# A state-space scan and a squared-ReLU FFN on one core: two weight loads re-ordered among GpSimd's work, and the third block's down-projections written closer behind its up-projections

## The chip, the cores and the metric

The kernel runs on one core of one Trainium2 chip. The metric is device time in microseconds (us) for one execution; lower is better. Four compute engines take part, each with its own queue of instructions that it works off in order: TensorE (matmuls; PE in the profile, its weight loads PEld), VectorE (DVE), ScalarE (ACT) and GpSimd (POOL). SyncE (SP) computes nothing; it issues most of the DMA transfers, also in order. GpSimd issues the weight loads.

## What is computed

For each of 4 batches and 8 heads, a decayed linear recurrence runs over 768 positions; its output, 3072 rows of 256, goes through a feed-forward layer. Cut to what matters:

```
log_a = log(clip(a, 1e-6, 1))
for each chunk of 32 positions:
    cum   = cumsum(log_a)                      # within the chunk
    M     = (C @ B.T) * exp(cum_i - cum_j) * causal
    y     = M @ x  +  (C @ state) * exp(cum)
    state = exp(sum(log_a)) * state  +  (B * exp(cum_last - cum)).T @ x
h   = relu(y_rows @ w_in)                      # w_in: 256 x 2048
out = (h * h) @ w_out                          # w_out: 2048 x 256
```

The inputs are float32; the matmuls run on bfloat16. The chunk length of the reference is not kept: the kernel works in longer pieces.

## The kernel before

**Units.** The work is cut into 12 units, one for each batch and each third (256 positions) of the sequence, numbered 0 to 11 over the batches first. A unit is loaded as three tiles, C, B and x (`ph_load`, line 123), and prepared: C and B, scaled by the running products of a, are written side by side into a bfloat16 tile `jt` (`prep_c`, line 169, and `prep_b`, line 177), and x is multiplied by the inverse products into `xs` (`prep_x`, line 189). The products stand in `P_sb`, their inverses in `Pinv`; `inv` (line 648) fills `Pinv` a few columns at a time with reciprocals on VectorE. `jt` is transposed into `bct`: by TensorE for units 0 to 3 (line 207, copied out of PSUM at lines 220 and 222), by a DMA transpose that SyncE issues for units 4 to 11 (`dma_tr`, line 198).

**A unit on TensorE.** The scores of a unit (`ph_mt`, line 231 or 237) fill PSUM banks 0 to 3 and are masked into `mts` (line 246; some are copied by ScalarE at line 251 and masked at line 255). Then come the unit's own state contribution (`ph_u`), the part inside the unit (`ph_intra`) and the carry from earlier states (`ph_carry`); all three are matmuls at line 262. The carry reads `Sd`, a state times its decay, which GpSimd makes at line 378 (`ph_sd`) or VectorE at line 390 (`ph_sd_first`). ScalarE copies the state contribution to `us` (lines 343 and 346). From unit 4 on, one region `rg` does this in a fixed order: carry of the unit before, state contribution of the new one, inside part of the unit before, scores of the new one. `rg4` is the first of them: it finishes unit 3 and starts unit 4. Its first matmuls are the carry of unit 3.

**The feed-forward layer.** The 256 rows of one unit form a block, called a to l (a belongs to unit 0). A block has 8 up-chunks of 256 hidden columns, in ORDER written `a0` to `a7`: four matmuls with `w_in` at line 453, then a relu by ScalarE (line 474). `qa0` squares the chunk on VectorE (line 480). The capital `A0` is the down-chunk: four matmuls with `w_out`, also at line 453, which add into one accumulator bank for the block (bank 6 for block b, bank 7 for the others). Down-chunk 7 comes last in every block, and with it goes the block's end: `mm2(blk, 7)` is followed at once by `ph_out`, which puts a ScalarE copy of the accumulator (line 502) and an output store on SyncE (line 503) into the queues.

**The order.** Nothing is scheduled by a planner. The string `ORDER` (line 48) is a list of tokens, read from left to right; each token emits its instructions to its engine, and that is the order in which each engine works. Tokens that the text below needs, beside the chunks: `ld`, `ldC5:s` and so on, loads on SyncE; `wi0` to `wi3` and `wo0` to `wo3`, the four loads each of `w_in` and `w_out` by GpSimd (lines 150 and 154), each holding the weights of two chunks; `iv`, reciprocals into `Pinv`; `pc`, `pb`, `px`, the preparations of C, B and x; `tr`, the transpose; `tc`, its copies; `mt`, scores; `mk`, `sc`, `ms`, masks; `u`, `in`, `ca`, `sf`, `us`, `t`, the parts of a unit (state contribution, inside part, carry, first decayed state, and the copies to `us` and to `T`, the block's input); `sa`, decayed states on GpSimd; `id`, filler matmuls on ones (line 554) that keep TensorE busy while nothing else is ready. A number behind `@` picks the PSUM bank; without it the next free bank in turn is taken. The loads of a unit wait for nothing but a free buffer, or a small gate that VectorE or GpSimd writes.

In the stretch that matters here, TensorE works through blocks a, b and c while units 2 to 4 are loaded and prepared. The helper `after` (line 670) lets GpSimd copy one column of a loaded tile, so that what GpSimd issues next comes behind that load.

Of the kernel before, what the change touches and what calls it, by code (L numbers as in the profile page):

```python
# [10 lines left out]
FP32 = mybir.dt.float32  # L11
# [12 lines left out]
def _dap(base: bass.AP, offset_elems: int, dims):  # L24

    return bass.AP(tensor=base.tensor, offset=base.offset + offset_elems,
                   ap=[list(d) for d in dims])
# [3 lines left out]
def kernel(  # L31
# [15 lines left out]
    NU = 12  # L47
    ORDER = """
        fa1:a jz0:v ef jz1:p id3:512 ti fa0:s la0:s id4:512 pi eb ldB0:s ac0:v ldC0:a sk0 ku sp la1:a pbh0:p hd
        id1:256 pc0:v pbl0:v mb:a id2:512 trC0 ps iv:8:16 tcC0:1:a tcC0:0:v trB0 la2:s tcB0:2:v pk id1:512 iv1:0:8  # L50
        id1:512 ldx0:s mt0 wi0 la3:s px0:v ldC1:s su id2:512 ldB1:s wi1 ldx1:s u0:67 mk0 fq mk0 gC2:v mk0 ac1:v pc1:p sc0
        pb1:a jz2:a id2:512 tr1 id3:512 tc1:1:a tc1:0:v to ms0:p sf0 sk1 wo0 wi2 px1:p mt1 ina0 inb0 ca0 pp1:a mk1 mk1 t0:aa
        sc1 us0 mk1 fr p2@4 a0 ldC2:s a1 u1::6 ina1 ms1:v wo1 wi3 pc2 inb1 sf1 ca1 pd t1:va us1 a3@0 qa1 ldB2:s
        qa0 a2@1 wo2 b0@2 qa3 qb0 b1@3 qb1 b2@4 b3@5 A0 A1 B0 pb2:p B1 tr2 zb0 qb3 gB3:v ldx2:s ldB3:s ldC3:s ldx3:s b4 a4
        iv:32:64 zb1 tc2:1:v qa2 tc2:0:v b5 sb1 sb0 qb4 a5 qb2 qa4 mt2 sc2 B3 iv:16:32 px2 pc3 wo3 px3 mk2 mk2 sc2 A3
        A2 ms2:v ms2:v qa5 a6 b6 pb3:a B2 a7 qb5 qa6 b7 u2 ina2 inb2 sf2 ld4 A4 tr3 ca2 tc3:1:v t2:aa B4 us2 B5
        tc3:0:v u3:45 pc4 mt3 A5 us3 sc3 c5 qb7 qb6 mk3 za3 pb4 ldC5:s ldB5:s c3 qa7 c4 qc5 c0 qc3 px4 tr4 ldx5:s pb5
        pc5 sa3 c1 c6 ldC6:s tr5 ldB6:s ldx6:s qc4 qc0 A6 px5 pq A7 wm c2 B6 c7 C0 ms3:v mk3 qc6 mk3 qc7 afC2 pc6 B7
        C3 C6 C4 qc1 bk rg4 C1 qc2 d1 d0 za4 sa4 pb6 mk4 mk4 d3 mk4 C5 d4 qd0 d2 mk4 px6 tr6 ld7 C2 C7 qd1 qd2 qd3 zb3
        rg5 sb3 D0 mk5 za5 sa5 D1 mk5 d5 qd4 D2 pc7 pb7 d6 qd5 d7 qd6 D3 zb2 e0 qd7 mk5 e1 qe0 sb2 D4 mk5 D5 tr7 ld8  # L60
        e2 qe1 D6 e3 qe2 ml px7 rg6 e4 D7 qe3 za6 sa6 zb6 mk6 e5 qe4 sb6 e6 qe5 e7 qe6 iv:64:96 mk6 E0 E1 E2 E3 ldC9:s
        ldB9:s px8 mk6 f0 qe7 E4 f1 qf0 pc8 E5 pb8 tr8 ldx9:s E6 mk6 f2 qf1 f3 qf2 E7 rg7 mk7 F0 f4 qf3 za7 F1 F2 f5
# [12 lines left out]
    const = ctx.enter_context(tc.tile_pool(name="const", bufs=1))  # L75
# [29 lines left out]
    Pinv = const.tile([128, 2, 96], FP32, name="Pinv")  # L105
# [34 lines left out]
    def gate(k, what, eng=None):  # L140
        b, j = UNITS[k]
        w = {"B": N, "C": N, "x": D}[what]
        t = nat.tile([128, NH, 2 * w], FP32, tag=f"{what}_nat", name=f"{what}_nat{k}")
        loaded.setdefault(k, {})[what] = t
        (eng or nc.gpsimd).memset(t[:, 0, 0:1], 0.0)

    def load_w_in(i):
        f0, f1 = WIN[i]
        n = (f1 - f0) * 256
        nc.gpsimd.dma_start(out=w_in_b[i], in_=_dap(moe_w_in, f0 * 256, [[2048, 128], [128 * 2048, 2], [1, n]]))  # L150

    def load_w_out(i):
        f0, _ = WOUT[i]
        nc.gpsimd.dma_start(out=w_out_b[i].rearrange("p s d -> p (s d)"),
                            in_=_dap(moe_w_out, f0 * 65536, [[1024, 128], [1, 1024]]))
# [303 lines left out]
    def mm1(blk, fp, h=None):  # L459

        if h is None:
            h = bank()
        gi, o = group_of(WIN, fp)
        w = w_in_b[gi]
        for i in range(2):
            for g in range(2):
                col = g * w.shape[2] + (o // 2) * 512 + 2 * (o % 2) + i
                strips(pp[:, h, i * 256:(i + 1) * 256], lambda c, n: _fap(w, col + 4 * c, [[4, n]]),
                       T[blk][:, g].rearrange("p r u t -> p (r u t)"), start=(g == 0), stop=(g == 1))
        return h  # L470

    def relu(blk, fp, h):
        hb = fpool.tile([128, 2, 256], BF16, tag="hb", name=f"hb{blk}_{fp}")
        nc.scalar.activation(out=hb.rearrange("p i t -> p (i t)"), in_=pp[:, h, :], func=AF.Relu)  # L474
        hbs[(blk, fp)] = hb
# [59 lines left out]
    with tc.manual_schedule():  # L535
# [3 lines left out]
        V, P, A, SQ = nc.vector, nc.gpsimd, nc.scalar, nc.sync  # L539
# [111 lines left out]
        def first_a(u, eng):  # L651
            load_a(u, eng)
# [15 lines left out]
        def after(what, k):  # L668
            t = const.tile([128, 1], FP32, name=f"gate_{what}{k}")
            P.tensor_copy(out=t, in_=loaded[k][what][:, 0, 0:1])  # L670

        def order_load(k, what):
            gate(k, what)

# [88 lines left out]
        def one(t):  # L763
            t, _, w = t.partition("@")
            want[:] = [int(h) for h in w]
            f = t.split(":")
            name = f[0].rstrip("0123456789")
            k = int(f[0][len(name):] or 0)
            if len(name) == 1 and name.lower() in "abcdefghijkl" and len(f[0]) == 2:
                blk = "abcdefghijkl".index(name.lower())  # L770
                if name.islower():
                    relu(blk, k, mm1(blk, k))
                else:
                    mm2(blk, k)
# [7 lines left out]
            {  # L782
                "a": lambda: None,
                "fa": lambda: first_a(k, eng),
                "la": lambda: late_a(k, eng),
                "ldC": lambda: load(k, "C", eng, f[1] if len(f) > 2 else None),
                "ldB": lambda: load(k, "B", eng, f[1] if len(f) > 2 else None),
                "ldx": lambda: load(k, "x", eng, f[1] if len(f) > 2 else None),
                "ld": lambda: load_all(k),
                "gC": lambda: gate(k, "C", eng), "gB": lambda: gate(k, "B", eng), "gx": lambda: gate(k, "x", eng),  # L790
                "afC": lambda: after("C", k), "afB": lambda: after("B", k), "afx": lambda: after("x", k),
                "wi": lambda: load_w_in(k), "wo": lambda: load_w_out(k),
                "id": lambda: idle(k, f[1], dep(f[2]) if len(f) > 2 else None),
                "ef": lambda: eye(eye_f, ones_f), "eb": lambda: eye(eye_b, ones_b[:, 0:128]), "wm": warmed, "hd": head_rows,
                "jz": lambda: cleared(jt[k], eng), "ti": triangle, "ml": later_mask, "pi": picks, "ku": quads,
                "mb": lambda: causal(eng), "pk": picked, "ac": lambda: clamp(k, eng), "sk": lambda: scan(k), "sp": first_p, "pp": lambda: second_pick(eng),
                "su": first_sums, "to": first_total, "fq": first_quad, "p": lambda: second_p(), "pd": second_copy, "pq": second_quad,
                "ps": lambda: A.copy(out=P_sb[:, :, 0:32], in_=P0.rearrange("p (r c) -> p r c", r=2)),
                "iv": lambda: inv(int(f[1]), int(f[2]), k == 1),
                "pc": lambda: prep_c(k, eng or P, P0 if k == 0 else None),  # L800
                "pb": lambda: prep_b(k, eng or P), "pbl": lambda: prep_b(k, eng, (0,)), "pbh": lambda: prep_b(k, eng, (1,)),
                "px": lambda: prep_x(k, eng or P),
                "tr": lambda: transpose(k, "") if k < 4 else dma_tr(k),
                "trC": lambda: transpose(k, "C"), "trB": lambda: transpose(k, "B"),
                "tc": lambda: trc(k, "", f[1], eng), "tcC": lambda: trc(k, "C", f[1], eng), "tcB": lambda: trc(k, "B", f[1], eng),
                "mt": lambda: scores(k), "mk": lambda: mask_direct(k) if k < 4 else next_mask(k), "sc": lambda: score_copy(k),
                "ms": lambda: mask_copied(k, eng),
                "u": lambda: first_u(k, f[1] if len(f) > 1 else None, f[2] if len(f) > 2 else None), "sf": lambda: ph_sd_first(k),
                "ca": lambda: ph_carry(k, live[k]["h"], live[k]["begun"]),
                "in": lambda: intra(k, ""), "ina": lambda: intra(k, "a"), "inb": lambda: intra(k, "b"),  # L810
                "t": lambda: region_t(k, f[1]), "us": lambda: region_us(k),
                "cm": lambda: cols.append(True), "rg": lambda: rg(k), "bk": late_banks, "fr": lambda: busy.discard(4),
                "za": lambda: ph_z(k, 0), "zb": lambda: ph_z(k, 1), "sa": lambda: ph_sd(k, 0), "sb": lambda: ph_sd(k, 1),
            }[name]()
# [59 lines left out]
```

## Time and profile before

| | us |
|---|---|
| median of 3 runs | 113.69 |
| lowest and highest | 113.65, 114.04 |
| the profiled execution | 113.69 |
| its span, first to last instruction | 112.0 |
| TensorE busy in it | 107.1 |
| VectorE, ScalarE, GpSimd busy | 83.0, 77.0, 49.3 |

The profile is one execution seen by the hardware profiler. A row of a timeline gives the start and the length in us from the span's start, the engine, the line of the kernel, the operation, output `<-` inputs, how many instructions are merged, and in brackets how long the engine stood idle before and what released it. The release is inferred: of several things waited for, the one that came last by the profile is named. Matmuls overlap, so a row's length holds the end of its last matmul; the distance between the starts of two rows is the time that the work takes. A transfer has two times, the time that its issue takes on the queue of its engine, and the time from issue to landing.

### The profile page before, as it was taken

Reading aid. Unit: us, or ns where it says so; the run is one execution under the profiler, and the core shown is the slowest. Engines: PE = TensorE matmul, PEld = TensorE weight load, DVE = VectorE, ACT = ScalarE, POOL = GpSimd, SP = SyncE. Lnnn points to the kernel's source line nnn. Section 1 sums busy time; section 2 is a strip of 40 time slices with the busy share of each in tenths; the row PEclk is TensorE's granted clock in tenths of the full one; section 3 lists DMA queues with packets and bytes.
Section 4 is the critical chain, followed back from the end, with each engine's and each line's share of the span. In section 5 each row is a group of like instructions: output and inputs, shape, how many; then the busy total and the mean of one; then the engine's idle time right before and its main releaser. Section 6 shows DMA issues by size and latency. Waiting matters only on the chain.

```text
span 112.0 us, 3688 instructions
## 1 busy us (share of the span) xinstructions
PE 107.1 (96%) x1453; PEld 91.8 (82%) x1453; DVE 83.0 (74%) x190; ACT 77.0 (69%) x159; POOL 49.3 (44%) x95
## 2 busy tenths in 40 slices
PE   6989999999899999999999999999999999999990
PEld 2436789878798989989989989899899899899980
DVE  1799768998973999979967998679598298355440
ACT  1767994876974776695677776877876867867840
POOL 7599464097565473494083960665420020000000
PEclk9999999999999999999999999999999999999999
DMA  1999999999689799998888877888940020010203
GB/s 37 202 208 136 184 205 216 165 200 186 98 173 119 81 288 77 130 162 89 118 152 115 187 110 85 189 102 113 168 117 0 6 97 0 33 61 6 94 0 94
DMA packets 67281, 13.44 MB, mean 120 GB/s; under 512 B 63104, under 2 KB 65984, under 8 KB 67264
## 3 DMA queue, kind: packets, MB, share of 16 engines
q1 hardware_dynamic: 64320, 10.88, 60.4%
q0 software_dynamic: 1664, 2.10, 11.6%
q10 hardware_dynamic: 1280, 0.23, 1.1%
q8 instruction: 11, 0.18, 0.7%
q14 instruction: 6, 0.05, 0.1%
HBM read 10.58 MB, written 3.15 MB: 123 GB/s over the span
## 4 chain that ended last, share of the span: by engine, by line
PE 72%; DMA 14%; POOL 5%; DVE 4%; issue 1%; SPq 1%; ACT 0%; POOLq 0%; ACTq 0%
PE pp L453 64%; DMA w_out_b<-in_moe_w_out_dram 11%; PE pp L262 5%; DMA B_nat<-in_B_dram 3%; PE pp L231 2%; DVE h L480 2%; POOL jt L169 2%; POOL w_in_b L150 1%; POOL xs L189 1%; DVE mts L246 1%; POOL mts L255 1%; PE pp L237 1%; DVE bct L222 1%; SPq L656 0%; SPq L119 0%
## 5 line engine op out<-in xcount | busy, mean ns | idle before, releaser
L474 ACT ACTIVATE hb<-pp 128x512 bf16<-128x512 f32 x96 | 54.5, 603 | 22.5 <-PE pp L453 20.6
L480 DVE TENSOR_TENSOR h<-hb 128x512 bf16<-128x512 bf16 x96 | 45.1, 486 | 13.2 <-ACT hb L474 12.9
L453 PE MATMUL pp<-w_out_b,h 128*128 128x256 bf16 (+1 forms) x400 | 53.8, 268 | 0.6 <-DMA w_out_b<-in_moe_w_out_dram 0.4
L453 PE MATMUL pp<-T,w_in_b 128*128 128x256 bf16 x384 | 53.3, 273 | 0.0
L453 PEld LDWEIGHTS <-w_in_b 128*128 128x128 bf16 x384 | 41.4, 114 | 1.8 <-issue 1.1
L453 PEld LDWEIGHTS <-h 128*128 128x128 bf16 x400 | 37.6, 98 | 5.4 <-issue 1.9
L246 DVE TENSOR_TENSOR mts<-pp,mask 128x512 bf16<-128x512 f32 x43 | 28.5, 676 | 0.8 <-PE pp L231 0.8
L189 POOL TENSOR_TENSOR xs<-x_nat,Pinv 128x256 bf16<-128x256 f32 (+1 forms) x19 | 13.8, 739 | 13.4 <-PE pp L262 4.6
L378 POOL TENSOR_TENSOR Sd<-z,Pquad 128x256 bf16<-128x256 f32 x16 | 10.6, 669 | 12.9 <-DVE z L362 8.9
L169 POOL TENSOR_TENSOR jt<-C_nat,P_sb 128x128 bf16<-128x128 f32 x22 | 9.8, 466 | 9.6 <-DMA C_nat<-in_C_dram 9.4
L362 DVE SCALAR_TENSOR_TENSOR z<-z,Ptot,us 128x64 f32<-128x64 f32 x8 | 3.0, 371 | 6.8 <-ACT us L346 4.6
L554 PE MATMUL pp<-const-bfloat16-1.0 128*128 128x512 bf16 (+1 forms) x19 | 6.4, 465 | 0.8 <-PEq L858 0.8
L502 ACT COPY osb<-pp 128x512 f32<-128x512 f32 x11 | 6.4, 583 | 1.0 <-PE pp L453 1.0
L177 POOL CAST jt<-B_nat 128x256 bf16<-128x256 f32 x9 | 4.1, 458 | 3.5 <-PE pp L453 3.2
L262 PE MATMUL pp<-mts,xs 64*32 64x128 bf16 (+1 forms) x288 | 5.4, 219 | 0.0
L262 PE MATMUL pp<-bct,Sd 128*128 128x128 bf16 x40 | 4.2, 220 | 0.3 <-DVE Sd L390 0.2
L262 PEld LDWEIGHTS <-xs 64*32 64x32 bf16 (+1 forms) x288 | 3.6, 93 | 0.4 <-issue 0.2
L262 PEld LDWEIGHTS <-Sd 128*128 128x128 bf16 x40 | 3.0, 98 | 0.9 <-DVE Sd L390 0.6
L554 PEld LDWEIGHTS <-const-bfloat16-1.0 128*128 128x128 bf16 x19 | 1.7, 112 | 2.4 <-issue 2.2
L150 POOL DMA_DIRECT2D w_in_b<-in_moe_w_in_dram x4 | 3.0, 759 | 0.2 <-issue 0.2
L251 ACT CAST sc<-pp 128x512 bf16<-128x512 f32 x5 | 2.9, 608 | 0.4 <-PE pp L237 0.3
L262 PEld LDWEIGHTS <-jt 64*32 64x32 bf16 (+1 forms) x128 | 1.5, 90 | 1.9 <-issue 0.8
(78 smaller groups left out, 57.7 us busy)
## 6 DMA issues: line engine op xcount, KB each, us to landing
out_dram<-osb SPq DMA_DIRECT2D x11, 256.0 KB, 2.9
x_nat<-in_x_dram SPq DMA_DIRECT2D x6, 256.0 KB, 4.9
w_in_b<-in_moe_w_in_dram POOLq DMA_DIRECT2D x4, 256.0 KB, 7.0
w_out_b<-in_moe_w_out_dram POOLq DMA_DIRECT2D x4, 256.0 KB, 6.8
B_nat<-in_B_dram SPq DMA_DIRECT2D x6, 128.0 KB, 4.4
C_nat<-in_C_dram SPq DMA_DIRECT2D x12, 64.0 KB, 3.5
B_nat<-in_B_dram SPq DMA_DIRECT2D x12, 64.0 KB, 2.9
x_nat<-in_x_dram SPq DMA_DIRECT2D x6, 128.0 KB, 2.9
```

The source lines that it names most:

```text
L150: nc.gpsimd.dma_start(out=w_in_b[i], in_=_dap(moe_w_in, f0 * 256, [[2048, 128], [128 * 2048, 2], [1, n]]))
L169: eng.tensor_tensor(out=_fap(jt[k % 3], 128 + 144 * g, [[384, 2], [32, 4], [1, 16]]), in0=_fap(loaded[k]["C"], 128 * g, [[16, 2], [32, 4], ...
L177: fn(out=_fap(jt[k % 3], 0, [[384, 2], [16, 2], [32, 4], [1, 16]]), in_=_fap(loaded[k]["B"], 0, [[16, 2], [128, 2], [32, 4], [1, 16]]))
L189: eng.tensor_tensor(out=_fap(xs, 256 * r, [[256, 2 // n], [32, 8], [1, 32]]), in0=_fap(loaded[k]["x"], 32 * r, [[32, 2 // n], [64, 8], [1, ...
L246: nc.vector.tensor_tensor(out=live[k]["mts"][:, q].rearrange("p r g i -> p (r g i)"), in0=pp[:, q, :], in1=mask1 if k >= LATE else mask, o ...
L262: nc.tensor.matmul(dst, w, v, start=bool(need), stop=False, skip_group_check=True, **({} if pos is None else {"tile_position": pos}))
L378: nc.gpsimd.tensor_tensor(out=_fap(S_d, 0, [[128, 2], [32, 4], [1, 32]]), in0=_fap(z, 0, [[32, 2], [0, 4], [1, 32]]), in1=_fap(Pquad, 4 * ...
L453: nc.tensor.matmul(dst, w(0, 128), v, skip_group_check=True, **flags)
L474: nc.scalar.activation(out=hb.rearrange("p i t -> p (i t)"), in_=pp[:, h, :], func=AF.Relu)
L480: nc.vector.tensor_tensor(out=h2, in0=hb, in1=hb, op=ALU.mult)
L502: nc.scalar.copy(out=osb, in_=pp[:, 6 if blk == 1 else 7, :])
L554: nc.tensor.matmul(pp[:, h, 0:int(cols)], ones_b[:, 0:128], ones_b[:, 0:int(cols)] if dep is None else dep, start=True, stop=True, skip_gr ...
```

## The change

Two lines of code are added, and tokens are moved in ORDER.

1. A new token `hold` stands ahead of `wi0`, the first load of `w_in`. It lets GpSimd copy one column of `Pinv`, column 8, which the reciprocals `iv:8:16` write.
2. One filler is shortened: `id2:512` (two matmuls of 512 columns) becomes `id1:384` (one of 384), ahead of the first unit's transposes.
3. `wo3`, the last load of `w_out`, moves ahead of `px2` (the third x) and `pc3` in GpSimd's order.
4. The chunks of blocks a, b and c are written in another order. A4, B4, A5 now stand ahead of unit 2's state contribution `u2`, then B5, A6, B6; A7 stands behind c0 and B7 behind c3. The up-chunks of block c go c0 c3 c4 c6 c5 c1 c2 c7, with banks given by `@`; C0, C3, C4 and C6 follow two up-chunks behind their own, and none of them is left between c7 and `rg4`. The squares move with them; `us3` is written ahead of the scores `mt3`.

With A7 and B7 their copies and stores move too: A7 from behind `ldx6` to ahead of `ldC5`, B7 from there to ahead of `tr4`.

The diff, with the unchanged lines around it left out:

```diff
-        id1:256 pc0:v pbl0:v mb:a id2:512 trC0 ps iv:8:16 tcC0:1:a tcC0:0:v trB0 la2:s tcB0:2:v pk id1:512 iv1:0:8
-        id1:512 ldx0:s mt0 wi0 la3:s px0:v ldC1:s su id2:512 ldB1:s wi1 ldx1:s u0:67 mk0 fq mk0 gC2:v mk0 ac1:v pc1:p sc0
+        id1:256 pc0:v pbl0:v mb:a id1:384 trC0 ps iv:8:16 tcC0:1:a tcC0:0:v trB0 la2:s tcB0:2:v pk id1:512 iv1:0:8
+        id1:512 ldx0:s mt0 hold wi0 la3:s px0:v ldC1:s su id2:512 ldB1:s wi1 ldx1:s u0:67 mk0 fq mk0 gC2:v mk0 ac1:v pc1:p sc0
...
-        iv:32:64 zb1 tc2:1:v qa2 tc2:0:v b5 sb1 sb0 qb4 a5 qb2 qa4 mt2 sc2 B3 iv:16:32 px2 pc3 wo3 px3 mk2 mk2 sc2 A3
-        A2 ms2:v ms2:v qa5 a6 b6 pb3:a B2 a7 qb5 qa6 b7 u2 ina2 inb2 sf2 ld4 A4 tr3 ca2 tc3:1:v t2:aa B4 us2 B5
-        tc3:0:v u3:45 pc4 mt3 A5 us3 sc3 c5 qb7 qb6 mk3 za3 pb4 ldC5:s ldB5:s c3 qa7 c4 qc5 c0 qc3 px4 tr4 ldx5:s pb5
-        pc5 sa3 c1 c6 ldC6:s tr5 ldB6:s ldx6:s qc4 qc0 A6 px5 pq A7 wm c2 B6 c7 C0 ms3:v mk3 qc6 mk3 qc7 afC2 pc6 B7
-        C3 C6 C4 qc1 bk rg4 C1 qc2 d1 d0 za4 sa4 pb6 mk4 mk4 d3 mk4 C5 d4 qd0 d2 mk4 px6 tr6 ld7 C2 C7 qd1 qd2 qd3 zb3
+        iv:32:64 zb1 tc2:1:v qa2 tc2:0:v b5 sb1 sb0 qb4 a5 qb2 qa4 mt2 sc2 B3 iv:16:32 wo3 px2 pc3 px3 mk2 mk2 sc2 A3
+        A2 ms2:v ms2:v qa5 a6 b6 pb3:a B2 a7 qb5 qa6 b7 qb6 A4 B4 A5 u2 ina2 inb2 sf2 ld4 B5 tr3 ca2 qb7 tc3:1:v t2:aa A6 us2 B6
+        tc3:0:v qa7 u3:45 pc4 us3 mt3 sc3 c0@4 mk3 za3 A7 pb4 ldC5:s ldB5:s c3@5 qc0 B7 c4@0 C0 qc3 c6@1 px4 tr4 ldx5:s pb5
+        pc5 sa3 qc4 C3 c5@4 wm qc6 ms3:v C4 c1@5 ldC6:s tr5 ldB6:s ldx6:s mk3 px5 pq c2@0 C6 qc5 mk3 c7@1 qc7 afC2 pc6
+        qc1 bk rg4 C1 qc2 d1 d0 za4 sa4 pb6 mk4 mk4 d3 mk4 C5 d4 qd0 d2 mk4 px6 tr6 ld7 C2 C7 qd1 qd2 qd3 zb3
...
+        def hold():
+            t = const.tile([128, 1], FP32, name="gate_inv")
+            P.tensor_copy(out=t, in_=Pinv[:, 0, 8:9])
...
+                "hold": hold, "wi": lambda: load_w_in(k), "wo": lambda: load_w_out(k),
```

More of the change, by code (lines that the diff above doesn't have):

```diff
@@ L791, in one @@
                 "afC": lambda: after("C", k), "afB": lambda: after("B", k), "afx": lambda: after("x", k),
-                "wi": lambda: load_w_in(k), "wo": lambda: load_w_out(k),
+                "hold": hold, "wi": lambda: load_w_in(k), "wo": lambda: load_w_out(k),
                 "id": lambda: idle(k, f[1], dep(f[2]) if len(f) > 2 else None),
```

## The prediction

> **What bounds the kernel now.** I read the page first, then the table of stretches, then TensorE's own timeline, and only then the queues that feed it. The profiled execution took 113.69 us, the same as the median of the three runs (113.65 to 114.04); its span is 112.0, so 1.69 us lie outside and I leave them as they are.
>
> ```profile
> span 112.0 us, 3688 instructions
> ```
> ```profile
> 36.00:112.00 76.00, 73.06 (x913) 66.35 (x912) 54.75 (x120) 52.55 (x103) 25.87 (x47) 1.00 0.62 99
> ```
>
> The second row is the stretch from 36 us to the end: TensorE (first pair) is busy 73.06 of 76.00 us at the full granted clock (1.00). Nothing waits there that could be given back, so a microsecond won or lost before 36 us is won or lost in the total. The change lies wholly before 36 us, so I read TensorE there. The columns are start, length, engine, line, form and count, with the idle time before and what ended it.
>
> ```profile
> 23.62 0.25 PE L262 MATMUL pp<-xs,jt 64*32 64x64 bf16 x16
> ...
> 26.82 0.61 PE L453 MATMUL pp<-w_out_b,h 128*128 128x256 bf16 x4
> 27.27 2.78 PE L453 MATMUL pp<-T,w_in_b 128*128 128x256 bf16 x24
> 30.50 1.03 PE L453 MATMUL pp<-w_out_b,h 128*128 128x256 bf16 x8 [0.45 <-DMA w_out_b<-in_moe_w_out_dram]
> ...
> 32.25 0.60 PE L453 MATMUL pp<-T,w_in_b 128*128 128x256 bf16 x4
> ...
> 34.87 0.28 PE L262 MATMUL pp<-bct,Sd 128*128 128x128 bf16 x2
> ...
> 35.58 0.42 PE L237 MATMUL pp<-bct 32*64 32x256 bf16 x16
> 35.94 0.61 PE L453 MATMUL pp<-w_out_b,h 128*128 128x256 bf16 x4
> ...
> 39.88 0.39 PE L262 MATMUL pp<-bct,Sd 128*128 128x128 bf16 x4
> ```
>
> One chunk of either projection is four matmuls; from 26.82 to 27.27 that is about 0.44 us. The 24 matmuls at 27.27 therefore occupy 2.62 us and TensorE could go on at 29.89; it goes on at 30.50. That 0.61 us is the wait for the last w_out, which GpSimd issues late:
>
> ```profile
> 24.47 5.99 DMA w_out_b<-in_moe_w_out_dram
> ```
> ```profile
> PE pp L262 <- DVE Sd L390: 0.2, 1, 0.2
> PEld L207 <- DVE jt L169: 0.2, 1, 0.2
> ```
>
> The first wait row is a second stall, a carry behind its decayed state (0.2 us). So this change has some 0.8 us to win in its second half.
>
> **Gains, and the small terms.** The third x is prepared on GpSimd after a long pause, and the state us3 is copied on ScalarE:
>
> ```profile
> 22.22 1.21 POOL L189 TENSOR_TENSOR xs<-x_nat,Pinv 128x512 bf16<-128x512 f32 x1 [3.32 <-DVE mts L255]
> ```
> ```profile
> 26.65 0.27 ACT L343 COPY us<-pp 128x128 f32<-128x128 f32 x1 [0.59 <-PE pp L262]
> ```
>
> The last w_out moves ahead of that x, from 24.47 to 18.90, where the pause of 3.32 begins. Landing 6 us later, at 25, it is there before A6, which now follows the region of unit 2 (23.62) and four chunks, so comes after 25.4: minus 0.61. B5 and the transposes now lie between the decayed state and its carry, about 0.8 us of cover: minus 0.2. The shorter filler is worth nothing: the transposes behind it already wait for VectorE (second wait row), and the 640 columns that go (0.27 us, by 0.44 for a chunk's 1024) are a shorter pause than the 0.45 us at 30.50, which the clock bore at 1.00. The written order puts c0, right behind the scores of unit 3, into the bank that us3 empties. us3 ended at 26.92, and TensorE, free at 26.82, would now wait for it: plus 0.16, with 0.06 for the semaphore (an estimate, between the 0.04 and the 0.1 from an end to the next engine's start further down).
>
> The hold makes GpSimd wait for the reciprocal and copy one column before the first w_in:
>
> ```profile
> 5.18 0.25 DVE L648 RECIPROCAL Pinv<-P_sb 128x16 f32<-128x16 f32 x1 [0.20 <-ACT P_sb L798]
> ```
> ```profile
> 5.37 1.63 POOL L150 DMA_DIRECT2D w_in_b<-in_moe_w_in_dram  x2 [0.24 <-issue]
> 7.14 0.76 POOL L169 TENSOR_TENSOR jt<-C_nat,P_sb 128x128 bf16<-128x128 f32 x2
> ...
> 36.05 0.19 POOL L670 COPY gate_C<-C_nat 128x1 f32<-128x1 f32 x1
> ```
> ```profile
> 7.69 0.40 ACT L177 CAST jt<-B_nat 128x256 bf16<-128x256 f32 x1 [0.73 <-DMA B_nat<-in_B_dram]
> ```
>
> The table is there at 5.43; plus 0.06 and a copy of 0.19 (line 670 copies the same one column) the first w_in starts at 5.7, or 5.95 if the 0.24 pause repeats: 0.3 to 0.6 later. Queued behind are the second w_in, the C preparation at 7.14 and everything GpSimd issues after. The second unit's transposes wait for the later of that preparation (7.90, now 8.2 to 8.5) and the B copy on ScalarE (8.09), so they move by 0.1 to 0.4. A gain is excluded, since the preparation cannot end earlier. I take plus 0.15: the first issue's share of the 1.63 may shrink behind the hold, which puts the low end nearer.
>
> So far: minus 0.61, minus 0.20, plus 0.16, plus 0.15, which is minus 0.50. TensorE would be ready for the fourth region (rg4, at 34.87) at 34.37.
>
> **The term that decides: two stores moved past SyncE's loads.** A7 and B7 each end a block, and the last chunk of a block also issues its ScalarE copy and its output store on SyncE. Before, A7 stood behind the x load of unit 6. Now A7 stands ahead of the C and B loads of unit 5, and B7 ahead of the transpose of unit 4. SyncE works in written order, and does wait for such copies:
>
> ```profile
> SPq L503 <- ACT osb L502: 22.3, 3, 7.6
> ```
> ```profile
> 25.29 1.98 SPq L136 DMA_DIRECT2D B_nat<-in_B_dram  x1
> 27.44 3.46 SPq L198 DMA_TRANSPOSE bct<-jt  x1
> 30.95 0.56 SPq L136 DMA_DIRECT2D x_nat<-in_x_dram  x1
> 31.57 1.33 SPq L131 DMA_DIRECT2D C_nat<-in_C_dram  x2
> ...
> 38.35 1.18 SPq L503 DMA_DIRECT2D out_dram<-osb  x2
> ```
>
> So the B load of unit 5, issued at 25.29 so far, must wait for the store of block A. When is that? From c0 to rg4 the new order has 14 chunks, 14 times 0.437 or 6.1 us: c0 at 28.25, A7 at 28.7, its result at 29.3 (a chunk's row lasts 0.60). ScalarE has c0's relu ahead of the copy. Before, the copy stood 0.04 behind the end of A7 (30.50 plus 1.03), and took 0.58:
>
> ```profile
> 31.57 0.58 ACT L502 COPY osb<-pp 128x512 f32<-128x512 f32 x1 [0.56 <-PE pp L453]
> ```
>
> It ends at 30.0. The store issues at 30.05 for 0.59 (half of 1.18), C at 30.65, B at 31.25. How long B then takes:
>
> ```profile
> DMA to landing us min/median/max: 3.0/3.1/3.3
> ```
> ```profile
> DMA to landing us min/median/max: 6.2/6.2/6.2
> ```
> ```profile
> DMA to landing us min/median/max: 2.6/2.8/2.9
> ```
>
> These are the first two B loads, when little else was under way; unit 5's B of 25.29, amid the weights; and unit 6's half-size B at 35 to 37. The queues will have drained by 30 us, as the loads stood still, so I take 3.1: landing 34.35, against 31.5 before. Who waits for it:
>
> ```profile
> 31.59 0.40 POOL L177 CAST jt<-B_nat 128x256 bf16<-128x256 f32 x1 [1.73 <-PE pp L453]
> ...
> 32.84 0.61 POOL L378 TENSOR_TENSOR Sd<-us,Pquad 128x256 bf16<-128x256 f32 x1
> ```
>
> GpSimd's copy started 0.1 after the landing, and 1.86 us after that the decayed state of unit 3 was ready (33.45), queued behind unit 5's two preparations. rg4's first matmuls are that state's carry, and TensorE cannot step over them. Now: 34.45, ready at 36.31, carry at 36.37. Against 34.87 that is **plus 1.50**, with the minus 0.50 already inside. The bounds: 2.6 us of flight and stores and loads that issue as quickly as the early ones give plus 0.4; 6.2 us would give plus 4.6, which an emptied queue makes unlikely.
>
> Inside this wait lies a second one, worth nothing while the first stands. c7 is now last before rg4, and c1's square is queued behind c7's on VectorE:
>
> ```profile
> 33.57 1.10 DVE L480 TENSOR_TENSOR h<-hb 128x512 bf16<-128x512 bf16 x3 [0.71 <-ACT hb L474]
> ```
>
> From c7's start (32.25) to the second of these squares (34.33) is 2.08 us; the work from c7 to C1 is 0.44 plus 1.07 (34.87 to 35.94). C1 would stand 0.62 with the semaphore, were rg4 on time.
>
> **The transpose and the next region.** The store of block B follows B's load, then the transpose of unit 4 at about 32.45 instead of 27.44. Transposes landed in:
>
> ```profile
> DMA to landing us min/median/max: 2.8/4.6/5.3
> ```
>
> That gives 37.05; the scores that read it come 0.71 into rg4, at 37.08. It just fits. SyncE then gets to unit 5's x and unit 6's C after 0 to 3.46 us more, C at 33.0 to 36.5 instead of 31.57. GpSimd waits for that C, and the carry of the fifth region stands behind it:
>
> ```profile
> 36.51 0.76 POOL L169 TENSOR_TENSOR jt<-C_nat,P_sb 128x128 bf16<-128x128 f32 x2 [0.27 <-DMA C_nat<-in_C_dram]
> 37.23 0.61 POOL L378 TENSOR_TENSOR Sd<-z,Pquad 128x256 bf16<-128x256 f32 x1
> ```
>
> Its state, ready at 37.84 so far, moves by 1.4 to 4.9, to 39.2 to 42.7; the carry would be due at 39.88 plus 1.5, 41.4. A wait of 0 to 1.3; I take 0.3. Sum: 1.50 and 0.30 are **plus 1.8, 115.5 us**.
>
> The Trainium skill (DMA: Bandwidth & Descriptors, section Anatomy of one DMA) fits a transfer, for GpSimd's issues, as 2.0 us plus its bytes at 436 GB/s. For 128 KB that is an estimate of 2.3 us, and the sum by it would be plus 1.0, 114.7. The first B loads took 3.0 to 3.3 here, so I stay with the row.
>
> **Rivals.** (1) Not slower: the late B does no harm, because it lands before GpSimd's copy is needed. The state is ready 2 us after the landing, so this holds if B lands by 32.3, a flight of 1.1 us after the issue at 31.25. The rows have nothing under 2.6 for a load of its kind; it takes a store that does not hold the loads up, that is, a change that does not put them in the order it says. Then the 0.62 at C1 comes out: 113.69 minus 0.50 plus 0.62, 113.8. 0.12 for that; 0.04 for a gain of over half a percent, which needs the squares in time and the hold for nothing as well (113.0).
>
> (2) Slower still: the last w_out starves the third x. While weights were queued, from 13.5 to 18 us, the two queues moved:
>
> ```profile
> q0 software_dynamic: 653, 0.82, 103.8%
> q1 hardware_dynamic: 500, 0.10, 15.1%
> ```
>
> Columns: packets, MB, share. 0.82 MB in 4.5 us is 0.18 MB a microsecond, so the last w_out's 0.26 MB takes 1.4 us, and x may be late by that. The region of unit 2 was due at 23.62, and now has A4, B4 and A5 (1.3 us) ahead of it. Up to about 1.5 us of delay is covered; beyond that each microsecond costs one. At 2.4 us, 0.9 comes on top: 116.4. I give it 0.10.
> The Trainium skill (DMA: Bandwidth & Descriptors, section Queues, rings and completion order) says that a DMA engine takes its queues in turn, a packet each. That speaks against moving a weight load ahead of x. The trace agrees: 653 packets against 500 in these rows, with eight times the bytes.
>
> **How the numbers follow.** The forecast's mechanism has 0.74, at 115.5; with rival 2, 0.84 for slower, 0.12 for no change, 0.04 for faster. Half a percent, 0.57 us, is about what a measurement of this kernel can tell from no change. The range runs from plus 0.5 (fast flights) to plus 3.1 (rival 2, and the next region's wait at its upper end): 114.2 to 116.8.
>
> **What would show it.** In the changed profile SyncE should have a store at line 503 at about 30, unit 5's C and B behind it, and a gap in its issues before. GpSimd's copy at line 177 should start near 34.4 instead of 31.59, and TensorE should stand about 2 us before the carry at line 262 with GpSimd's Sd as releaser. The 0.45 us before A6 should be gone. I am wrong if B is issued near 25 after all, or if TensorE runs into rg4 without a wait; if it stands for xs of unit 2, rival 2 holds.

## The result and the profile after

| | before | after |
|---|---|---|
| median, us | 113.87 | 117.1 |
| lowest and highest, us | 113.65, 121.55 | 116.39, 117.35 |
| the profiled execution, us | 113.69 | 117.35 |
| its span, us | 112.0 | 115.6 |

The ratio of after to before is 1.0255 (95% interval 1.0208 to 1.0302): slower by 2.9 us on 113.87, between 2.4 and 3.4. Ratios, here and below, leave out executions over 1.5% above the fastest of the same kernel (none of the four after and one of the four before; below, six of twelve in stores_late and masks_first_hold, three of six in no_hold, four of six in unit2_b_on_act), so they can differ from the quotient of two medians. The forecast was slower, 115.5 us, with a range of 114.2 to 116.8. 1.0255 times its 113.69 is 116.6, inside; the median of 117.1 lies 0.3 above the upper end.

The hold is three lines of code, 672 to 674 of the changed kernel; `ph_out` and everything before it keep their numbers. From the page, and from the table of stretches:

```profile
span 115.6 us, 3682 instructions
```
```profile
38.00:116.00 78.00, 73.84 (x944) 66.71 (x931) 56.35 (x120) 52.88 (x103) 27.95 (x49) 1.00 0.60 96
```

Behind 38 us TensorE is busy 73.84 of 78.00 us, at the same granted clock; before, it was 73.06 of 76.00 behind 36. The window reaches 0.4 past the end of the span, and one wait of 1.0 us in it comes below; without these two it is as full as before. The rest of the loss lies ahead of it. SyncE's timeline shows its cause (start, length of the issue, line, output `<-` input):

```profile
24.73 0.98 SPq L136 DMA_DIRECT2D x_nat<-in_x_dram  x1
31.12 0.37 SPq L503 DMA_DIRECT2D out_dram<-osb  x1
31.59 0.38 SPq L136 DMA_DIRECT2D C_nat<-in_C_dram  x1
32.02 0.70 SPq L136 DMA_DIRECT2D B_nat<-in_B_dram  x1
32.81 0.89 SPq L503 DMA_DIRECT2D out_dram<-osb  x1
33.81 1.41 SPq L198 DMA_TRANSPOSE bct<-jt  x1
35.28 1.50 SPq L136 DMA_DIRECT2D x_nat<-in_x_dram  x1
36.84 1.70 SPq L131 DMA_DIRECT2D C_nat<-in_C_dram  x2
```
```profile
SPq L503 <- ACT osb L502: 26.8, 5, 7.6
```

SyncE issues nothing between 25.71 and 31.12. It stands at the store of block A, which waits for ScalarE's copy; unit 5's C and B are queued behind it, and unit 4's transpose behind the store of block B. The wait row (total, times, longest) has 26.8 us in 5 waits where before had 22.3 in 3. ScalarE's timeline has the copy, and GpSimd's has those who wait for B:

```profile
30.51 0.58 ACT L502 COPY osb<-pp 128x512 f32<-128x512 f32 x1
```
```profile
35.45 0.40 POOL L177 CAST jt<-B_nat 128x256 bf16<-128x256 f32 x1 [5.45 <-DMA B_nat<-in_B_dram]
35.80 0.76 POOL L169 TENSOR_TENSOR jt<-C_nat,P_sb 128x128 bf16<-128x128 f32 x2
36.52 0.79 POOL L378 TENSOR_TENSOR Sd<-us,Pquad 128x256 bf16<-128x256 f32 x1
40.03 1.19 POOL L189 TENSOR_TENSOR xs<-x_nat,Pinv 128x256 bf16<-128x256 f32 x2 [2.72 <-PE pp L453]
...
41.74 0.95 POOL L169 TENSOR_TENSOR jt<-C_nat,P_sb 128x128 bf16<-128x128 f32 x2
42.66 0.79 POOL L378 TENSOR_TENSOR Sd<-z,Pquad 128x256 bf16<-128x256 f32 x1
```

The cast at 35.45 had 5.45 us of idle GpSimd before it; before, it ran at 31.59. The decayed state of unit 3 is done at 37.31. Then GpSimd stands 2.72 us before it prepares unit 5's x, and from there it works without a pause to the state that the fifth region reads (42.66 plus 0.79). The row at 40.03 names TensorE; that x, issued at 35.28, landed at 39.88, and in the profiles of store_b_late and no_hold (below) the same row is released by it. TensorE's timeline:

```profile
12.40 1.07 PE L453 MATMUL pp<-T,w_in_b 128*128 128x256 bf16 x8 [0.95 <-DMA w_in_b<-in_moe_w_in_dram]
...
29.32 0.60 PE L453 MATMUL pp<-T,w_in_b 128*128 128x256 bf16 x4
...
35.00 0.60 PE L453 MATMUL pp<-T,w_in_b 128*128 128x256 bf16 x4
37.37 0.28 PE L262 MATMUL pp<-bct,Sd 128*128 128x128 bf16 x2 [1.77 <-POOL Sd L378]
...
42.39 0.28 PE L262 MATMUL pp<-bct,Sd 128*128 128x128 bf16 x2
43.51 0.28 PE L262 MATMUL pp<-bct,Sd 128*128 128x128 bf16 x2 [0.84 <-POOL Sd L378]
```

c7 starts at 35.00 and takes 0.44, so TensorE was ready for rg4 at 35.44 and stood 1.93 us. In the fifth region the second half of the carry follows its first half after 1.12 us, where before both ran as one row of x4 (halves 0.11 apart): another 1.0. Between the two, 42.39 minus 37.37 is 5.02 us, as before (39.88 minus 34.87). So 2.93 us of new waits stand against 2.9 measured. The difference of the two spans, 3.6, has besides: A0 came 1.27 later (17.02 against 15.75), and from A0 to rg4 without its wait 0.70 went away (18.42 against 19.12). About 0.1 is left over.

### The profile page after: what moved, and what is told of

It is laid out like the page before. It is cut to its first block, busy times and chain, and to the rows that moved or that the text cites. A ratio compares the mean times of both kernels' runs of the same rounds, so it can differ in the third digit from the quotient of the medians.

```text
span 115.6 us, 3682 instructions
## 1 busy us (share of the span) xinstructions
PE 107.7 (93%) x1452; PEld 92.2 (80%) x1452; DVE 84.1 (73%) x190; ACT 77.2 (67%) x159; POOL 50.1 (43%) x96
## 4 chain that ended last, share of the span: by engine, by line
PE 78%; DMA 8%; POOL 4%; DVE 3%; ACT 2%; issue 1%; SPq 1%; ACTq 0%; POOLq 0%
PE pp L453 66%; PE pp L262 6%; DMA w_in_b<-in_moe_w_in_dram 6%; DMA B_nat<-in_B_dram 3%; PE pp L554 3%; PE pp L231 2%; DVE mts L246 2%; POOL jt L169 1%; POOL Sd L378 1%; PE pp L237 1%; PE pp L207 1%; ACT hb L474 1%; PE pp L531 1%; ACT us L343 0%; DVE jt L169 0%
## 5 line engine op out<-in xcount | busy, mean ns | idle before, releaser
L474 ACT ACTIVATE hb<-pp 128x512 bf16<-128x512 f32 x96 | 55.0, 602 | 23.1 <-PE pp L453 22.3
L480 DVE TENSOR_TENSOR h<-hb 128x512 bf16<-128x512 bf16 x96 | 46.5, 503 | 13.1 <-ACT hb L474 12.7
L453 PE MATMUL pp<-T,w_in_b 128*128 128x256 bf16 x384 | 54.1, 273 | 1.0 <-DMA w_in_b<-in_moe_w_in_dram 0.9
L378 POOL TENSOR_TENSOR Sd<-z,Pquad 128x256 bf16<-128x256 f32 x16 | 11.4, 725 | 8.4 <-DVE z L362 6.0
L554 PE MATMUL pp<-const-bfloat16-1.0 128*128 128x512 bf16 (+2 forms) x18 | 6.7, 498 | 0.8 <-PEq L862 0.8
L362 DVE SCALAR_TENSOR_TENSOR z<-z,Ptot,us 128x64 f32<-128x64 f32 x8 | 2.4, 299 | 6.6 <-ACT us L346 5.0
L329 ACT CAST T<-pp 128x512 bf16<-128x512 f32 x3 | 1.8, 585 | 3.4 <-PE pp L262 3.4
```

Source lines behind the costliest of these rows:

```text
L378: nc.gpsimd.tensor_tensor(out=_fap(S_d, 0, [[128, 2], [32, 4], [1, 32]]), in0=_fap(z, 0, [[32, 2], [0, 4], [1, 32]]), in1=_fap(Pquad, 4 * ...
L453: nc.tensor.matmul(dst, w(0, 128), v, skip_group_check=True, **flags)
L480: nc.vector.tensor_tensor(out=h2, in0=hb, in1=hb, op=ALU.mult)
L554: nc.tensor.matmul(pp[:, h, 0:int(cols)], ones_b[:, 0:128], ones_b[:, 0:int(cols)] if dep is None else dep, start=True, stop=True, skip_gr ...
```

## The experiments

Three theories were tried against one another. S: the two stores hold SyncE's loads up. H: the hold costs the time, by a later first w_in (the row at 12.40 above is its evidence). W: the last w_out, issued earlier, starves x. To move a store alone, the output store at line 503 was cut from `ph_out` into a function of its own, with a token `st0` or `st1` for block a or b, while its ScalarE copy stays where it was:

```diff
+    kept, LATER = {}, (0, 1)
...
+        kept[blk] = osb
+        if blk not in LATER:
+            send(blk)
+
+    def send(blk):
+        b, j = UNITS[blk]
+        osb = kept.pop(blk)
```

Of the lines of ORDER only the tokens around an edit are shown. All kernels were timed in five rounds, in three groups; the kernel before, run among them, had medians of 114.1, 113.76 and 114.16.

**Both stores late** (from the kernel after):

```diff
-  ldC6:s tr5 ldB6:s ldx6:s mk3 px5
+  ldC6:s tr5 ldB6:s ldx6:s st0 st1 mk3 px5
```

> The changed kernel with one thing put back: the output stores of blocks a and b are issued on SyncE behind the x load of unit 6 again, as before the change; their ScalarE copies and every chunk stay where the change put them. Theory S (the two stores hold up the loads behind them): the stands before the fourth and fifth region (1.9 and 1.0 us of TensorE in the changed profile) go, B of unit 5 is issued before 28 us, and C1 now stands about 0.6 us behind the squares, so the time falls by some 2.3 us, to a ratio of about 1.008 to the kernel before. Theory H (the hold in front of the first w_in is what costs): less than 0.5 us falls, ratio 1.02 or more. Theory W (the early last w_out starves the third x): less than 0.5 us falls, and TensorE stands before the state contribution of unit 2.

Measured: 115.16 us median, ratio to the kernel before 1.0027 (0.9986 to 1.0069). SyncE's and TensorE's timelines:

```profile
27.14 0.84 SPq L136 DMA_DIRECT2D B_nat<-in_B_dram  x1
```
```profile
36.65 0.27 PE L262 MATMUL pp<-bct,Sd 128*128 128x128 bf16 x2
36.85 0.25 PE L262 MATMUL pp<-xs,jt 64*32 64x64 bf16 x16
36.92 0.65 PE L262 MATMUL pp<-mts,xs 64*32 64x128 bf16 x32
37.50 0.42 PE L237 MATMUL pp<-bct 32*64 32x256 bf16 x16
38.30 0.61 PE L453 MATMUL pp<-w_out_b,h 128*128 128x256 bf16 x4 [0.37 <-DVE h L480]
```

Unit 5's B is issued at 27.14 (25.29 before) and the carry has no wait in its row. With the stores out of the way, 2.3 of the 2.55 per cent are gone: S holds, and the ratio is lower than the 1.008 expected. By the two medians, 115.16 against 114.1, 0.9 per cent would be left. The profiled execution took 116.06 us; it lost time ahead of the change's stretch, where the transposes of unit 2 stood for a late B:

```profile
19.97 0.51 PE L207 MATMUL pp<-eye_b,jt 128*128 128x128 bf16 x6 [1.30 <-POOL jt L177]
```

In the place of the first wait, near rg4, the second one appears, behind VectorE's square (L480): from the carry to C1 it is 1.65 us, against 1.07 before, so 0.58.

**One store late at a time**, `st0` or `st1` alone in that place, the other store left where the change put it:

```diff
-    kept, LATER = {}, (0, 1)
+    kept, LATER = {}, (0,)
```

> The changed kernel with the store of block a alone put back behind the x load of unit 6; the store of block b stays ahead of the transpose of unit 4. Theory S, taken store by store: C and B of unit 5 are issued before 28 us and the carry of the fourth region no longer waits for GpSimd's Sd; but the transpose of unit 4 cannot be issued before block b's copy ends near 31 to 32 us, lands some 4 us later, and TensorE now stands about 1 us before the scores in the fourth region, with the DMA transpose as releaser. Ratio to the kernel before 1.008 to 1.015, between 1.003 (both stores late) and 1.026 (neither). If the store of block a did no harm, the ratio stays at 1.02 or more.

> The changed kernel with the store of block b alone put back; the store of block a stays ahead of the C and B loads of unit 5. Theory S, store by store: the carry of the fourth region stands about 1.9 us as in the changed kernel, since B of unit 5 is still issued only near 32 us; the transpose comes one store (0.9 us of SyncE) earlier, so the stand before the fifth region shrinks from 1.0 to 0.3 us or less. Ratio 1.016 to 1.022. If the store of block b alone did the harm, the ratio falls to about 1.005.

Measured with store a late: 115.65 us, 1.0186 (1.0137 to 1.0235); with store b late: 116.65 us, 1.0258 (1.021 to 1.0305). TensorE's timeline of the first:

```profile
35.12 0.28 PE L262 MATMUL pp<-bct,Sd 128*128 128x128 bf16 x2
...
36.88 0.42 PE L237 MATMUL pp<-bct 32*64 32x256 bf16 x16 [0.97 <-DMA bct<-jt]
```

and of the second:

```profile
37.61 0.29 PE L262 MATMUL pp<-bct,Sd 128*128 128x128 bf16 x2 [1.67 <-POOL Sd L378]
...
42.63 0.39 PE L262 MATMUL pp<-bct,Sd 128*128 128x128 bf16 x4
```

Both ratios lie above what was expected (1.008 to 1.015, and 1.016 to 1.022). Store b ahead of the transpose is enough to make the scores of rg4 wait for the transpose; store a ahead of B is enough for the whole of the first wait. In both profiles the fifth region's carry is one row of x4 again (at 41.17 in the first), so that in these profiles the second wait of 1.0 us takes both stores. With store b late the profiled span is 0.8 shorter than the changed kernel's for it (114.8 against 115.6), but the timed ratio is not lower. The two prices do not add up: store b alone costs about 1.9 per cent, store a alone 2.6, both together 2.55.

**The hold.** Taken from the kernel after (no_hold), added to the kernel before (hold_only), and added to the best of the later versions (masks_first_hold, below):

```diff
-  id1:512 ldx0:s mt0 hold wi0 la3:s
+  id1:512 ldx0:s mt0 wi0 la3:s
```

> The changed kernel without the hold: GpSimd issues the first w_in as soon as it is free, all else stays as changed, the shorter filler too. Theory S as predicted (the hold is worth 0.15 us): the ratio to the kernel before falls by 0.001 to 0.002 only. Theory H: the first up-chunk goes back from 12.4 us to near 10.9 in the profile and the ratio falls by 0.008 to 0.013, since the first w_in lands as much earlier; the two stands before the regions stay at some 2 and 1 us.

> The kernel before with the hold alone added. If the hold costs what was predicted: plus 0.15 us, ratio 1.001, no change that can be measured. Theory H, from the changed profile (first up-chunk 1.5 us later, down-chunk A0 1.3 us later): plus 0.4 to 1.3 us, ratio 1.004 to 1.011, with the first w_in landing 0.5 us later or more and the copy on GpSimd of some 0.19 us ahead of its issue.

Measured: without the hold 117.92 us, 1.0245 (1.0161 to 1.0328), not measurably faster than the kernel after; with the hold alone 114.27 us, 1.0011 (0.9971 to 1.0051). H falls as the cause of the loss; the second run shows it, since the first has a loss of its own (below). TensorE's timeline of hold_only:

```profile
12.60 1.06 PE L453 MATMUL pp<-T,w_in_b 128*128 128x256 bf16 x8 [1.14 <-DMA w_in_b<-in_moe_w_in_dram]
...
28.77 2.78 PE L453 MATMUL pp<-T,w_in_b 128*128 128x256 bf16 x24
31.39 1.04 PE L453 MATMUL pp<-w_out_b,h 128*128 128x256 bf16 x8
```

The late first w_in is there (idle 1.14), as in the kernel after, and yet the time is not 1.3 us longer. One reason is in the last two rows: 28.77 plus the 2.62 of 24 matmuls is 31.39, so A6 does not wait for the last w_out here. What the start loses, the 0.61 of the old wait gives back in part.

no_hold also has a wide spread (116.15 to 122.33 us). Its profile shows a reason, in the table of stretches (the granted clock is the third number from the end) and TensorE's timeline:

```profile
36.00:38.00 2.00, 1.37 (x68) 0.89 (x69) 1.04 (x2) 0.68 (x2) 0.42 (x1) 0.97 1.08 182
38.00:40.00 2.00, 2.00 (x11) 1.45 (x10) 1.89 (x4) 0.42 (x2) 0.99 (x2) 0.50 1.08 145
40.00:42.00 2.00, 2.00 (x15) 1.57 (x13) 1.05 (x3) 1.45 (x3) 2.00 (x6) 0.68 0.78 80
```
```profile
38.56 2.77 PE L453 MATMUL pp<-T,w_in_b 128*128 128x256 bf16 x12
```

The granted clock (the 0.50 and 0.68) is at half from 37.87 to 41.28, after a wait of 1.85 us at rg4 that looks like the one of the kernel after: 12 matmuls take 2.77 us instead of 1.47. rg4's carry came 0.89 earlier than in the kernel after (36.48 against 37.37), but from there to the carry of the fifth region it took 6.91 us instead of the 5.02 that the kernel after takes there. The mean granted clock was 0.985 or 0.986 in four of the six executions of no_hold, and 0.985 in one of the four of the kernel after, so that this run alone does not price the hold.

**The last w_out alone** (from the kernel before), for theory W:

```diff
-  B3 iv:16:32 px2 pc3 wo3 px3
+  B3 iv:16:32 wo3 px2 pc3 px3
```

> The kernel before with one token moved: the last w_out ahead of the third x on GpSimd; chunks and stores as before. By the prediction's term: A6 waits no more, minus 0.61 us, ratio 0.995. Theory W (it holds up what SyncE loads behind the weights): the third x lands no later than 23 us, as in all profiles so far, but the fourth x lands 1.5 us later, at 26 instead of 24.5, and TensorE stands up to 1 us before the state contribution of unit 3, which has no chunks in front of it here: ratio 0.999 to 1.004.

Measured: 113.94 us, 1.0036 (0.9996 to 1.0077). The third x landed at 22.30 us, against 22.09 in the kernel before and 22.35 in the kernel after, so W falls: it is not starved. The fourth x, which the expectation has landing at 26 by W, did land at 25.67 (24.53 before), but 25.68 in hold_only too, where the last w_out stands in its old place, and TensorE did not stand for it. Nor is there a gain in the time. TensorE's timeline:

```profile
18.92 0.51 PE L207 MATMUL pp<-eye_b,jt 128*128 128x128 bf16 x6 [1.00 <-POOL jt L177]
```

In this execution the third B, loaded amid the weights, took 9.7 us (6.1 before) and its transposes waited 1.0 us for it.

**Repairs.** `mended` is the kernel after with both stores late, no hold, and c1's square ahead of c7's; `masks_first` has in addition both last masks of unit 3 ahead of the squares (the second new line):

```diff
-  ldx6:s mk3 px5 pq c2@0 C6 qc5 mk3 c7@1 qc7 afC2 pc6 qc1 bk rg4
+  ldx6:s st0 st1 mk3 px5 pq c2@0 C6 qc5 mk3 qc1 c7@1 qc7 afC2 pc6 bk rg4
...
+  ldx6:s st0 st1 mk3 mk3 px5 pq c2@0 C6 qc5 qc1 c7@1 qc7 afC2 pc6 bk rg4
```

> The changed kernel without the hold, with the stores of blocks a and b behind the x load of unit 6, and with the square of c1 ahead of the square of c7 on VectorE. Theory S together with the prediction's sum: what is left is the gain of 0.8 us (last w_out, carry) less 0.16 us (c0 behind us3) and up to 0.2 us (scores behind c7's relu), so 0.4 to 0.7 us faster than the kernel before, ratio 0.994 to 0.997. If the early last w_out itself costs (theory W), the ratio stays at or over 1.00 and TensorE stands before the state contribution of unit 2 or 3.

> As the mended kernel (changed kernel, no hold, both stores late, c1's square ahead of c7's), and with the last two masks of unit 3 ahead of c5's square on VectorE, so that neither the inside part of unit 3 (0.51 us stand in the mended kernel's profile) nor C1 (0.64 us in the profile with the stores late) waits in the fourth region. Expected: the fourth region runs without a stand over 0.25 us, and the ratio falls by about 0.004 below the mended kernel's, to 0.993 to 0.996. If the stands there were not what held the mended kernel at 0.998, it stays at 0.998.

> The version with both stores late, c0 and the last masks reordered, now with the hold as well. The theory that the hold trades one load for another: the second x lands by 9.5 us instead of 12.1 and w_in0 at 11.8 to 12.5 instead of 10.4 to 10.8, so the sum of the two is about nothing: ratio to the kernel before 0.995 to 1.001, no stand at region 4. The rival, that the hold is a cost of its own (0.15 us predicted, 1.3 us by the profiled run of the changed kernel): 1.002 to 1.012.

Measured: mended 114.16 us, 0.9981 (0.9937 to 1.0025); masks_first 113.82 us, 1.0009 (0.998 to 1.0039); masks_first with the hold 115.11 us, 1.0053 (1.0008 to 1.0099). In mended the inside part waits for a mask and an early transpose for the third B:

```profile
19.20 0.51 PE L207 MATMUL pp<-eye_b,jt 128*128 128x128 bf16 x6 [1.58 <-POOL jt L177]
```
```profile
36.67 0.41 PE L262 MATMUL pp<-mts,xs 64*32 64x128 bf16 x29 [0.30 <-DVE mts L246]
```

In masks_first the first of the two rows below waits for the second x, which landed 7.1 us after its issue, and little is left near rg4: from the carry to C1 it is 1.20 us (35.36 to 36.56) against 1.07 before:

```profile
13.33 0.25 PE L262 MATMUL pp<-xs,jt 64*32 64x64 bf16 x16 [1.06 <-POOL xs L189]
...
35.36 0.28 PE L262 MATMUL pp<-bct,Sd 128*128 128x128 bf16 x2
```

With the hold that x lands after 4.3 us, but the first w_in takes 6.8 instead of 5.5, and TensorE waits for it instead:

```profile
12.69 1.06 PE L453 MATMUL pp<-T,w_in_b 128*128 128x256 bf16 x8 [1.16 <-DMA w_in_b<-in_moe_w_in_dram]
...
35.72 0.28 PE L262 MATMUL pp<-bct,Sd 128*128 128x128 bf16 x2
```

The hold trades one late load for another and loses 0.36 us at rg4 in this pair of profiles; by the times, somewhere between nothing and half a per cent (1.0011 against 1, 1.0053 against 1.0009), and 1.1 in the last pair below, with wide intervals (1.0228 against 1.0121). None of the repaired versions is faster than the kernel before by more than its measurement can tell; mended and masks_first were expected at 0.993 to 0.997.

**The filler alone** (from the kernel before):

```diff
-  id1:256 pc0:v pbl0:v mb:a id2:512 trC0
+  id1:256 pc0:v pbl0:v mb:a id1:384 trC0
```

> The kernel before with only the filler shortened from 512 to 384 columns. By the prediction nothing: ratio 0.998 to 1.002. The rival, that the filler keeps TensorE busy until the clock is granted, so that a shorter one leaves the first matmuls at half clock for longer: full clock later than the 3.8 to 6.2 us seen so far, and a ratio of 1.003 to 1.008.

Measured: 114.0 us, 0.9997 (0.996 to 1.0033): nothing, as predicted. The clock record of the trace begins with full clock at 6.16 us, in the kernel after too, and at 3.77 before, but at 3.73 in no_hold, which also has the short filler; it moves from run to run, and no price of it shows in these times. This kernel has the old order of the blocks, and TensorE's timeline shows the same as hold_only:

```profile
28.18 2.78 PE L453 MATMUL pp<-T,w_in_b 128*128 128x256 bf16 x24
30.80 1.04 PE L453 MATMUL pp<-w_out_b,h 128*128 128x256 bf16 x8
```

28.18 plus 2.62 is 30.80: again no wait for the last w_out, which landed at 28.35 here and at 30.46 in the profiled execution of before. From A0 to rg4 the old order took 18.37 us here and 18.54 in hold_only; the new order, without its waits, 18.41 in masks_first, masks_first_hold and 18.42 in after.

**The third B from another queue** (from masks_first, with and without the hold): B of unit 2 is issued by ScalarE instead of SyncE.

```diff
-  tc1:1:a tc1:0:v to ms0:p
+  tc1:1:a tc1:0:v to ldB2:a ms0:p
...
-  us1 a3@0 qa1 ldB2:s
+  us1 a3@0 qa1
```

> The same version without the hold, but unit 2's B is issued from ScalarE's queue at about 9.3 us instead of SyncE's. If the third B comes late because it stands behind C in one row of transfers while the weights take their turns packet by packet, it now lands by 16 us in the profile, the second transpose stage has no stand over 0.4 us, and the ratio to the kernel before is 0.990 to 0.998. If it is starved by the weights whatever row it is in, it lands at 17 to 19.5 us as before and the ratio stays at 0.999 to 1.003.

> Both together: the third B from ScalarE's queue and the hold. If the early scatter is made of the second x and the third B, both land early (x by 9.5 us, B by 16 us), and the ratio is 0.988 to 0.997, with the gain of 0.7 us of the second half now in the time. If the hold's later w_in0 costs more than the x saves, it is 0.3% or more above the version without the hold.

Measured: 118.57 us, 1.0121 (1.0055 to 1.0187), and with the hold 116.76 us, 1.0228 (1.0173 to 1.0283). The theory that B is late because it queues behind C falls, and the other, which expected no change, is no better: alone in its row, B took 12.5 us instead of 8.1. TensorE's timeline, and the DMA rows of 12 to 18 us and of 18 to 22 us (packets, MB, share):

```profile
22.45 0.51 PE L207 MATMUL pp<-eye_b,jt 128*128 128x128 bf16 x6 [3.40 <-POOL jt L177]
```
```profile
q0 software_dynamic: 653, 0.85, 79.7%
...
q10 hardware_dynamic: 967, 0.12, 13.6%
```
```profile
q0 software_dynamic: 363, 0.49, 69.7%
...
q10 hardware_dynamic: 73, 0.01, 2.2%
```

q10 holds ScalarE's transfers. B is issued at 9.40, shows no packet until 12 us, has 967 of its 1040 packets by 18, and needs another 4 us for the last 73, while GpSimd's weights (q0) pass. The last packets set the landing. Why these few are left so long was not settled.
The Trainium skill (DMA: Bandwidth & Descriptors, section Queues, rings and completion order) has each DMA engine take its queue rows in turn, a packet at a time. From 12 to 18 us the trace agrees: B's row moved 967 packets and the weights' 653. On SyncE's row, in masks_first, the whole of B had landed by 17.1 us. The tail is not in that rule.

## Why the prediction was right, and where it was off

The direction and the mechanism were right. In the prediction's terms the 1.8 is 2.00 for the wait at rg4, minus 0.50 of gains and small terms, plus 0.30 at the next region. The profiles show 1.93, about nothing, and 1.0, together the 2.9 that was measured. The two misses point the same way, and the range held 116.6 by 0.2.

- **Stores ahead of loads, plus 1.50: right.** All its steps came about 1 us later than written, because everything from A0 on did: the store at 31.12 (predicted 30.05), B's issue at 32.02 (31.25), its landing 3.3 later at 35.3 (34.35), the cast at 35.45 (34.45), and 1.86 from the cast to the state, the carry at 37.37 (36.37). The wait itself was predicted at 2.00 (36.37 minus 34.37) and measured at 1.93. That the stores cause it is shown by both stores late. The transpose just fitted, as written: it landed at 38.02, and the scores start at 38.09.
- **The flight of B, 3.1: right by the row.** It took 3.3. The estimate of 2.3 by the Trainium skill (DMA: Bandwidth & Descriptors, section Anatomy of one DMA), which the prediction weighed and left, would have put the wait 0.8 lower.
- **The hidden wait at C1, 0.62: right in size.** Bared in the run with both stores late, it was 0.58, of which 0.14 (0.58 minus 0.44 for the inside part) fell to a mask.
- **The next region, 0.3 taken of 0 to 1.3: mis-sized, and by another load.** It was 1.0. The prediction let GpSimd wait for unit 6's C. That C landed at 40.49 and 40.86, and its reader, the copy at line 670, ran at 41.60 without a wait. GpSimd stood ahead of that, 2.72 us before it prepared unit 5's x, which lies between the transpose and that C on SyncE's queue and landed at 39.88 (whether the x or TensorE, which the row names, came last is not shown). The failing was to take a value near the lower end without a reason, and to let GpSimd wait for the C alone, where both stores and the transpose issue ahead of the x as well. This is 0.7 of the 1.1 by which 116.6 exceeds 115.5.
- **The last w_out, minus 0.61: wrong as an average.** The step took the wait at A6 of one execution for a property of the kernel. Two other profiles of the old order have no such wait, and moving w_out alone won nothing (1.0036). The last w_out landed at 30.46 before, 30.37 in hold_only and 28.35 in filler_only, while A0 started at 15.75, 17.22 and 16.80: with the quick start A6 waits; with the slower ones the wait is gone. Part of what is left of the gap lies here: the 0.70 that the pair of profiles shows from A0 to rg4 is 0.1 against hold_only and nothing against filler_only.
- **The carry, minus 0.20: read off the wrong row, and not a property of the kernel either.** At unit 2's carry, where the prediction puts the gain, the starts do show 0.21 in that execution (0.55 us from the transposes to the carry, 24.65 to 25.20, against 0.34 after, 27.23 to 27.57). But it is 0.34 in hold_only and filler_only as well, with the old order. The wait row shown for it is of an earlier carry, which the change leaves alone and which waits 0.24 in the kernel after too (at 14.28); TensorE's timeline of before:

```profile
12.72 0.28 PE L262 MATMUL pp<-bct,Sd 128*128 128x128 bf16 x2 [0.24 <-DVE Sd L390]
```

- **The hold, plus 0.15 (0.1 to 0.4): not settled.** Two pairs of times give 0 to half a per cent, one pair 1.1. The prediction priced the delay of GpSimd's queue. What the profiles show is another thing: with the hold alone, w_in0 was issued 0.5 later than before (5.87 against 5.37) and flew 1.35 longer (6.68 against 5.33), while the second x landed at 9.1 to 9.3 in every profile with the hold and at 9.5 to 12.3 in those without.
- **us3 ahead of c0, plus 0.16:** from the scores (28.83) to c0 (29.32) it is 0.49 in the profile after, where before A5 followed the scores by 0.35 (26.47 to 26.82): plus 0.14, right. **The filler, 0:** right.
- **The range: its upper end does not add up.** Rival 2 (0.9) and the next region's wait at its upper end (1.3) on top of 1.50 make plus 3.7, 117.4, and not the plus 3.1 that is written. The median of 117.1 lies between the two.
- **Rivals.** Rival 1 (no harm, 113.8) came true only once the stores were moved, as its condition says: B issued at 27.14 did no harm. Rival 2 (w_out starves x) fell: x at 22.35 against 22.09.

## What to carry to other kernels

When a chunk of compute is moved, list what it puts into the DMA-issuing queue too: a store that waits for its producer holds every load written behind it, and its price is that of the load's last reader, here 2 us for a store of 0.37. Issued behind the loads, the same stores gave 2.3 of the 2.55 per cent back. Before a wait of one profile is counted as a gain, look at another execution with a slower start: where the transfer does not land later as well, the wait shrinks by what was lost before it, as the 0.61 here did. A wait row of a whole profile names no time; find its row in the timeline before it is put into a sum.

## What the runs showed of the hardware that was not expected

- A wait of 1.85 us on TensorE was followed by half clock for 3.41 us in one profile (37.87 to 41.28, no_hold), while one of 1.93 in the kernel after and one of 3.56 in unit2_b_on_act (idle of 3.40 in its row) left it at 1.00. In unit2_b_on_act_hold half clock came during a wait of 3.35 (18.36 to 21.71) and held from 20.64 to 27.46 us, 6.83 us by the clock record; 16 matmuls that took 1.91 us elsewhere took 3.62. The Trainium skill (TensorE: Matmul & The Clock Gate, section What's actually happening) has a free-running window of 3.413 us, and half clock after at least one idle window. The lengths agree, one window and two; but here a wait of about half that length came before the half clock once. What decides between the four waits is open.
- A 128 KB load that travels beside GpSimd's weight loads takes 5.9 to 10.6 us on SyncE's queue from one execution to the next, and up to 12.5 on ScalarE's; one of the same size, unit 5's B in the kernel after, took 3.3 once the weights were through. The waits that this scatter makes (0.77 to 1.58 us at unit 2's B in four of the profiles, 1.06 at unit 1's x in masks_first) are about as long as, or longer than, the 0.8 us that the change set out to win.
